# Five 1 KB reads of k, v and the weights on the SP queue of an attention and channel-mix kernel

## The chip, the core and the metric

The kernel runs on one core of a Trainium2 chip. A core has a matrix engine (TensorE, PE in the profile), a vector engine (VectorE, DVE), a scalar engine (ScalarE, ACT), a general engine (GpSimd, POOL) and a queue engine (SyncE, SP) that issues transfers. ACT and POOL can issue transfers too. Sixteen DMA engines carry all transfers between the main memory and the core's working memory. The metric is the device time of one execution in microseconds, lower is better.

## The reference, cut to what matters

Attention without a score matrix, and behind it a channel mix. All inputs are float32: q, k, v of 8 batches x 8 heads x 576 positions x 64, two mixing vectors of 512, and three weights.

```python
q_s = softmax(q, axis=-1)                 # over the 64 of a head
k_s = softmax(k, axis=2)                  # over the 576 positions
kv  = einsum('bhsd,bhse->bhde', k_s, v)   # 64 x 64 for each head
x   = einsum('bhsd,bhde->bhse', q_s, kv)  # put together as 8 x 576 x 512
x_prev = x shifted by one position, a zero row first
xk = mu_k * x + (1 - mu_k) * x_prev
xr = mu_r * x + (1 - mu_r) * x_prev
k  = maximum(xk @ w_k, 0)                 # 512 -> 1024
v  = (k * k) @ w_v                        # 1024 -> 512
out = sigmoid(xr @ w_r) * v
```

w_k is 512 x 1024 (2 MB), w_v 1024 x 512 (2 MB), w_r 512 x 512 (1 MB).

## The kernel before, in words

**Tiling.** A batch's attention is done in two head groups g = 0 and 1 of four heads each (`attention`, L442). For each (batch, group) and each of q, k and v there is one raw tile of 128 x 2 x 576 float32 (576 KB), taken from twelve buffers raw_a to raw_l. Half u = 0 holds two neighbouring heads, half u = 1 the two heads that lie four further; for group 0 these are heads 0, 1 and heads 4, 5. ACT takes the exponentials of q (eq) and k (ek), POOL, ACT or DVE cast v to bf16 (vv), DVE sums and scales q (L467 to L475), PE transposes q (L507) and multiplies k by v (L484). For batches 0 and 1 the mixing with mu is folded into small weights (wp, L564), which need mu spread over all partitions (mu_all); PE multiplies them by q (L520), and DVE and ACT copy the results to xk and xr (L577).

**The channel mix** (`unit`, L694) goes over the positions in pieces of up to 512 columns: w_k matmuls (L722), ReLU on ACT (L706), square on DVE (L710), w_r matmuls (L756) with tanh on ACT (L761), w_v matmuls (L766), the product on DVE (L772), and the stores from SP (L783).

**Loads.** Batch 0's twelve half tiles of 288 KB are loaded from ACT's queue (the q tile of group 0) and from SP's (all others: k and v of group 0, then q, k and v of group 1), by `load` (L301) and the table `FIRST` (L32). SP first issues `emit_mu_rows_load` (L361), two reads of 2 KB each that PE spreads over the partitions (L367), ACT copies (L371) and POOL completes (L375). All other loads, the weights' (cast to bf16 in the transfer) and those of batches 1 to 7, are issued from POOL in the order of `LOADS` (L35) and, behind it, of the batches. The first of them waits until `first[GATE]` has landed, the second half of group 1's q tile (L37, L389, L829).

**The order of the work** comes from a planner (`Plan`, L72). Each operation is added with an engine, a planned time on the engine (`occ`), a planned latency, a key, its dependencies and the buffers it takes and gives. `order` (L133) starts every engine at 0.7 us and always takes the operation that can start first, by the due time (the key, or what its followers leave it) where several can within a look-ahead. Transfers keep their key as due time, so a lower key is an earlier place on the queue. The mu rows have -600 (L378), batch 0's loads -100 to -94.9. The plan treats a transfer of size under 20 as a small one that lands 2.2 us behind its planned end (if its key is negative) and takes no bandwidth; the others share one stream of 404 KB per us that begins 1.75 us behind the issue (`DMA_RATE`, `DMA_LEAD`, L191 to L197):

```python
            if op.size and op.size < 20:
                op.end += 2.2 if op.key < 0 else 6.0
            elif op.size:
                dma_free = max(dma_free, t + DMA_LEAD) + op.size / DMA_RATE
                op.end = dma_free + DMA_TAIL
```

The operations are then emitted sorted by planned start (L205, L827), so the planned times fix the order on each engine and nothing else; on the chip an engine waits for the semaphores of what it needs. Semaphores are assigned to the transfers of SP and ACT in the order of emission.

Of the kernel before, what the change touches and what calls it, by code (L numbers as in the profile page):

```python
# [12 lines left out]
F32 = mybir.dt.float32  # L13
# [195 lines left out]
def kernel(  # L209
# [14 lines left out]
    B, H, S, D = q.shape  # L224
# [16 lines left out]
    plan = Plan(pools, shared)  # L241

    const = ctx.enter_context(tc.tile_pool(name="const", bufs=1))
# [47 lines left out]
    pick = const.tile([2, 2, 64], F32, name="pick")  # L291
    mu_all = const.tile([128, 2, 2, 2, 128], F32, name="mu_all")
    warm = const.tile([1, 1], F32, name="warm")

    copies = {"ACT": nc.scalar.copy, "DVE": nc.vector.tensor_copy, "POOL": nc.gpsimd.tensor_copy}
    queues = {"SP": nc.sync, "ACT": nc.scalar, "POOL": nc.gpsimd}
# [44 lines left out]
    def emit_late_consts():  # L343
        for t in xbs:
            nc.vector.memset(t[:, :, 0:1], 0.0)

    zero = plan.add("DVE", 0.1, 0.15, -10, emit_warm_zero)
    plan.add("ACT", 1.55, 1.6, 3.5, emit_warm, [zero])
    identity = plan.add("POOL", 0.6, 0.8, -9.1, emit_identity)
# [74 lines left out]
    for h in range(2):  # L424
        wv_done.append(plan.add("POOL", 0.8, 0.8, LOADS.index(f"wv{h}"), lambda h=h: emit_wv(h), gate,
                                size=1200.0))
# [434 lines left out]
```

The softmax here doesn't subtract the row's maximum and nothing guards it: scores larger than these inputs give would overflow.

## Time and profile before

| what | us |
|---|---|
| median of 14 runs | 202.36 (201.02 to 203.27) |
| the profiled execution's own time | 201.30 |
| its span, first to last instruction | 199.4 |
| first transfer issued | 0.74 |
| last half of batch 0's group 1 q tile lands | 9.99 |
| first load issued from POOL | 10.29 |
| first w_k matmul (L722) starts | 17.60 |

The span is what the profiler's instructions cover; 1.9 us of the execution's time lie outside it. The profile is of one execution. Its views are: the page, with busy time by engine, the span in slices, the chain of work that ended last and the costliest groups; the windows, with busy time of each engine in a chosen stretch, the granted clock, the share of the DMA engines and GB/s; the waits, with who waited for whom; the instructions in order of time, in which a bracket tells how long the engine had been idle and what released it; and the trace's records of single DMA packets, with start, duration, size and queue, but without the engine or the tile. In a row such as `PE L722 MATMUL` L722 is the line of the kernel. Names ending in q (SPq) are the engines' queues, which issue transfers.

### The profile page before, as it was taken

How to read it: one execution, taken by the hardware profiler on the slowest of the kernel's cores; microseconds unless marked ns; L12 is line 12 of the kernel's file. 1: busy time of each engine (PE TensorE's matmuls, PEld its weight loads, DVE VectorE, ACT ScalarE, POOL GpSimd, SP SyncE). 2: the span in 40 equal slices, each digit the busy share in tenths (PEclk: the TensorE clock that was granted, in tenths of full speed). 3: DMA queues.
4: the chain of work that ended last, by engine and by line, in shares of the span. 5: the costliest groups of instructions: out<-in, count | busy, mean ns of one | idle time of the engine just before them, and what ended most of it. 6: DMA issues, size and time to landing. Idle time of an engine off the chain costs nothing.

```text
span 199.4 us, 5338 instructions
## 1 busy us (share of the span) xinstructions
PE 185.3 (93%) x2171; PEld 96.5 (48%) x2171; DVE 161.0 (81%) x348; ACT 137.3 (69%) x212; POOL 40.4 (20%) x66
## 2 busy tenths in 40 slices
PE   2548999999999999999999999999999999999992
PEld 0234554545444555454576455455455544544761
DVE  2498658898999999999979999999998997432531
ACT  5593795998999699979569978846842752552440
POOL 1494365733444123312300000000000000000000
PEclk9999999999999999999999999999999999999999
DMA  6999999999999999993991220251042204402514
GB/s 200 356 268 198 303 257 340 393 404 409 387 403 408 406 403 384 402 402 93 281 362 31 54 56 0 53 128 35 3 107 56 53 3 105 105 0 57 118 38 105
DMA packets 15520, 40.72 MB, mean 204 GB/s; under 512 B 2300, under 2 KB 3592, under 8 KB 15496
## 3 DMA queue, kind: packets, MB, share of 16 engines
q0 software_dynamic: 7840, 27.40, 40.2%
q1 hardware_dynamic: 7208, 12.26, 21.5%
q10 hardware_dynamic: 448, 0.72, 1.2%
q8 instruction: 17, 0.28, 0.5%
q14 instruction: 7, 0.06, 0.1%
HBM read 33.56 MB, written 9.44 MB: 216 GB/s over the span
## 4 chain that ended last, share of the span: by engine, by line
PE 82%; DMA 12%; DVE 1%; POOL 1%; ACT 0%; issue 0%; SPq 0%; DVEq 0%
PE mm_c L766 11%; PE mm_a L722 9%; PE mm_d L766 8%; PE mm_d L722 8%; PE mm_a L766 7%; PE mm_b L766 6%; PE mm_b L756 6%; PE mm_c L722 6%; PE mm_b L722 5%; DMA wk<-in_moe_w_k_dram 5%; PE mm_d L756 4%; PE mm_a L756 3%; DMA raw_d<-in_q_dram 3%; DMA raw_h<-in_k_dram 3%; PE mm_c L756 3%; PE att_b L520 2%
## 5 line engine op out<-in xcount | busy, mean ns | idle before, releaser
L722 PEld LDWEIGHTS <-wk 128*128 128x128 bf16 x320 | 35.4, 114 | 27.2 <-issue 1.5
L722 PE MATMUL mm_a<-xk,wk 128*128 128x512 bf16 (+1 forms) x100 | 24.5, 359 | 0.0
L722 PE MATMUL mm_d<-xk,wk 128*128 128x512 bf16 (+1 forms) x88 | 22.6, 370 | 0.0
L766 PEld LDWEIGHTS <-k_b 128*128 128x128 bf16 x152 | 14.5, 98 | 15.7 <-issue 0.7
L756 PEld LDWEIGHTS <-xr 128*128 128x128 bf16 x144 | 13.9, 98 | 15.9
L766 PEld LDWEIGHTS <-k_a 128*128 128x128 bf16 x144 | 13.4, 98 | 15.5 <-issue 0.4
L722 PE MATMUL mm_c<-xk,wk 128*128 128x512 bf16 (+1 forms) x68 | 16.4, 362 | 0.0
L722 PE MATMUL mm_b<-xk,wk 128*128 128x512 bf16 (+1 forms) x64 | 15.6, 353 | 0.0
L756 PE MATMUL mm_b<-wr_bf,xr 128*128 128x512 bf16 x52 | 13.4, 379 | 0.0
L766 PE MATMUL mm_c<-wv_bf,k_a 128*128 128x512 bf16 x48 | 12.4, 380 | 0.0
L766 PE MATMUL mm_c<-wv_bf,k_b 128*128 128x512 bf16 x48 | 12.3, 379 | 0.0
L761 ACT ACTIVATE th_a<-mm_b 128x512 f32<-128x512 f32 x12 | 7.1, 595 | 6.4 <-PE mm_b L756 5.3
L766 PE MATMUL mm_d<-wv_bf,k_b 128*128 128x512 bf16 x40 | 10.3, 380 | 0.0
L766 PE MATMUL mm_b<-wv_bf,k_a 128*128 128x512 bf16 x40 | 10.3, 379 | 0.0
L766 PE MATMUL mm_a<-wv_bf,k_b 128*128 128x512 bf16 (+1 forms) x40 | 9.4, 358 | 0.0
L756 PE MATMUL mm_d<-wr_bf,xr 128*128 128x512 bf16 x36 | 9.2, 379 | 0.0
L766 PE MATMUL mm_d<-wv_bf,k_a 128*128 128x512 bf16 x32 | 8.2, 380 | 0.0
L710 DVE TENSOR_TENSOR k_a<-rel_c 128x512 bf16<-128x512 bf16 (+1 forms) x13 | 5.0, 388 | 3.6 <-ACT rel_c L706 3.6
L710 DVE TENSOR_TENSOR k_a<-rel_b 128x512 bf16<-128x512 bf16 (+1 forms) x14 | 5.6, 397 | 2.7 <-ACT rel_b L706 2.7
L761 ACT ACTIVATE th_b<-mm_c 128x512 f32<-128x512 f32 x6 | 3.7, 609 | 5.6 <-PE mm_c L756 4.7
L756 PE MATMUL mm_c<-wr_bf,xr 128*128 128x512 bf16 x28 | 7.2, 379 | 0.0
L756 PE MATMUL mm_a<-wr_bf,xr 128*128 128x512 bf16 x28 | 7.2, 379 | 0.0
(275 smaller groups left out, 416.2 us busy)
## 6 DMA issues: line engine op xcount, KB each, us to landing
out_dram<-ot_a SPq DMA_DIRECT2D x24, 128.0 KB, 3.2
out_dram<-ot_b SPq DMA_DIRECT2D x24, 128.0 KB, 3.2
out_dram<-ot_c SPq DMA_DIRECT2D x22, 128.0 KB, 3.4
raw_b<-in_k_dram POOLq DMA_DIRECT2D x3, 576.0 KB, 8.9
raw_c<-in_v_dram POOLq DMA_DIRECT2D x3, 576.0 KB, 9.1
raw_d<-in_q_dram POOLq DMA_DIRECT2D x3, 576.0 KB, 10.6
raw_a<-in_q_dram POOLq DMA_DIRECT2D x2, 576.0 KB, 10.5
raw_e<-in_k_dram POOLq DMA_DIRECT2D x2, 576.0 KB, 12.3
```

Of the source, the lines that this page charges most:

```text
L520: nc.tensor.matmul(bank(xp)[64 * hf:64 * hf + 64, u, at + c:at + e], lhsT=w[r, hf, :], rhs=qts[qt.index][r, hf, src:src + e - c], start=(n ...
L710: nc.vector.tensor_tensor(out=k2s[k2.index][:, fc, 0:n], in0=rels[rel.index][:, 0:n], in1=rels[rel.index][:, 0:n], op=ALU.mult)
L722: nc.tensor.matmul(bank(kf)[:, 0:n], lhsT=(w[:, h, u, fc % 4:F // 2:4] if split[ct // 2] else w[:, u, F // 2 * h + fc % 4:F // 2 * (h + 1) ...
L756: nc.tensor.matmul(bank(rps), lhsT=xs[1][:, ct, c:c + 128], rhs=wr_bf[:, ct // 2 + 2 * (ct % 2), :], start=(ct == 0), stop=(ct == CT - 1))
L761: nc.scalar.activation(out=ths[th.index][:], in_=bank(rps), func=ACT.Tanh, scale=0.5)
L766: nc.tensor.matmul(bank(vps)[:, 0:w], lhsT=k2s[k2.index][:, ft, 128 * m:128 * m + 128], rhs=wv_bf[:, ft, e:e + w], start=(ft == 0), stop=( ...
```

## The change

A tile of 16 x 5 x 16 float32 is added that nothing reads. A function `touch` issues a read of 16 rows of 64 bytes into it. Five such reads go on SP's queue. Those of k and v have the keys -700 and -699, ahead of the mu rows; their rows lie 8 x 576 elements (18 KB) apart from the tensor's start, so they span the first 288 KB of each. Those of w_k, w_r and w_v have the keys -98.5, -98.49 and -98.48, behind the two halves of group 0's k tile (-99 and -98.9) and ahead of group 0's v tile (-98); their rows are spread over the whole weight, a sixteenth of it apart. Each has a planned time of 0.36 us on SP. The rest of the program text is the same, and no operation depends on the five.

```diff
+    touched = const.tile([16, 5, 16], F32, name="touched")
...
+    def touch(engine, i, src, step):
+
+        return queues[engine].dma_start(out=touched[:, i, :], in_=bass.AP(
+            tensor=src.tensor, offset=src.offset, ap=[[step, 16], [1, 16]]))
+
+    for i, src in enumerate((k, v)):
+        plan.add("SP", 0.36, 0.4, i - 700, lambda i=i, src=src: touch("SP", i, src, 8 * S),
+                 size=10.0)
+    for i, src in enumerate((moe_w_k, moe_w_r, moe_w_v)):
+        plan.add("SP", 0.36, 0.4, 0.01 * i - 98.5, lambda i=i, src=src: touch(
+            "SP", 2 + i, src, src.shape[0] * src.shape[1] // 16), size=10.0)
```

## The prediction

> **What bounds the kernel now.** I read the page's busy shares first, then the windows, then the waits of TensorE, then the chain that ended last, and only then the DMA issues of the first microseconds. The page says that PE is the bound and where it is not yet at work:
>
> ```profile
> span 199.4 us, 5338 instructions
> PE 185.3 (93%) x2171; PEld 96.5 (48%) x2171; DVE 161.0 (81%) x348; ACT 137.3 (69%) x212; POOL 40.4 (20%) x66
> PE   2548999999999999999999999999999999999992
> ```
>
> The third line is PE in 40 slices of 5 us: full from the fifth slice on. The windows put 9.6 us of PE's 14.1 us of idle time ahead of 17.5 us, 3.9 us behind 190 us, and 0.6 us between. So the end moves with the moment at which PE gets going, at 17.60 us with the first k matmul (L722); nothing behind it pays back or adds on its own as long as the loads keep pace. What leads to 17.60 us? The rows of ACT and DVE in time order:
>
> ```profile
> 9.27 1.42 ACT L454 ACTIVATE eq_b<-raw_d 128x576 bf16<-128x576 f32 x2 [1.49 <-DMA raw_d<-in_q_dram]
> ...
> 9.99 1.49 DVE L467 TENSOR_REDUCE rsum_b<-eq_b 128x9 f32<-128x576 bf16 x2 [2.49 <-ACT eq_b L454]
> ```
>
> The brackets are the idle time ahead of each: ACT stood 1.49 us until the q piece of head group 1 (raw_d) landed, DVE 2.49 us until ACT was through. From 9.99 us DVE is busy without a break (2.50 of 2.50 us from 10 to 12.5) up to the mixing weights and the xk copy that PE waits for at 16.50. So **the landing of raw_d is the anchor of the front end**: first half at 9.27, second at 9.99. The second also opens the gate of the POOL loads, as the chain that ended last shows (start, length, what):
>
> ```profile
> 4.03 5.96 DMA raw_d<-in_q_dram
> 9.99 0.30 issue
> 10.29 0.74 POOL raw_g L310
> 11.03 1.41 POOL wk L396 x2
> 12.44 9.08 DMA wk<-in_moe_w_k_dram
> ```
>
> wk's last part lands at 21.52 and PE's first matmul on it starts at 21.64: a margin of 0.12 us. Both paths hang on raw_d.
>
> What sets raw_d's landing is the stream of twelve 288 KB pieces. The windows (the last column is GB/s, the one before it the share of the 16 DMA engines):
>
> ```profile
> 3.50:4.50 1.00, 0.52 (x1) 0.50 (x2) 0.12 (x1) 0.73 (x2) 0.00 (x0) 1.00 1.07 364
> 4.50:5.50 1.00, 1.00 (x2) 0.00 (x0) 0.97 (x2) 0.63 (x1) 0.00 (x0) 1.00 0.93 228
> ...
> 10.50:11.50 1.00, 0.00 (x0) 0.00 (x0) 1.00 (x3) 0.88 (x2) 1.00 (x2) 1.00 1.03 403
> ```
>
> The engines are full from 2.5 us, yet move only 228 GB/s at 4.5 to 5.5 against 403 later. The packet records say why. A 2,304 B packet takes 93 ns, but among the 361 that start from 3.5 to 6.2 us 24 take over 200 (up to 1,115), 12 of 460 from 6.2 to 9.1, and none of 489 after that. The excess is 0.49 + 0.20 us averaged over 16 engines, but over 1 us for the worst one, and a piece lands with its worst engine. These are the first reads of k and v; q's own first reads (1.77 us) cost 14 slow packets of up to 527 ns, 0.23 us averaged. The change goes for these.
>
> One more view is needed, the waits of SP's queue, with its issues:
>
> ```profile
> SPq L310 <- DMA raw_b<-in_k_dram: 0.5, 1, 0.5
> SPq L310 <- DMA raw_a<-in_q_dram: 0.4, 1, 0.4
> ...
> 1.16 0.24 SPq L363 DMA_DIRECT2D mu_rows<-in_moe_mu_r_dram  x1
> 1.44 0.83 SPq L310 DMA_DIRECT2D raw_b<-in_k_dram  x2
> 2.32 0.90 SPq L310 DMA_DIRECT2D raw_c<-in_v_dram  x2
> 3.66 0.80 SPq L310 DMA_DIRECT2D raw_d<-in_q_dram  x2
> ```
>
> SP, issuing, stood 0.4 us from 3.22 to 3.66 for q's landing, which its loads don't read. By the instructions' operands the DMAs of SP and ACT together go round eight semaphores, and the ninth waits for the first to land. Five touches take five of these places.
>
> **The change part by part.** It removes no instruction. It adds five DMA issues on SP and five 1 KB reads, moves every later issue, and may remove slow packets.
>
> *Issues.* A touch has 16 rows; the nearest rows are 0.24 us (mu's second, 2 rows) and 0.36 to 0.43 (128 rows), with 0.05 between. I take 0.25 to 0.30, and 0.36 for SP's first. Before k: touch k 0.74, touch v 1.15, mu 1.45 and 1.73, k's halves at 2.0 and 2.45 to 2.9 (from 1.44 and 1.85). This costs nothing: q's two pieces fill the engines until 3.5 to 4.0, and k's data came at 3.5 at the earliest. The cover is about 0.5 us (2.0 plus about 1.0 from issue to first packet, as q's 0.74 to 1.77).
>
> mu's rows land some 0.5 us later. PE's product on them (L367) (2.04 us) then ends at about 6.45 instead of 6.02; ACT's copy (6.35) and POOL's two products (7.01) slip by up to 0.2, and POOL's casts of v behind them too. The first user is DVE at 13.93: nothing.
>
> *The ring.* By the planned starts the order is q, touch k, touch v, q, mu, mu, k, k: eight. The touch of w_k is the ninth and waits for q's first half (3.65 us). Queued behind it on SP are w_r, w_v, v, v, q, q, k, k, v, v, and everything on the critical path wants q among them. Three touches of 0.30: v's first half is issued at 4.6 instead of 2.32. It is the twelfth, and the fourth (q's second half, landed at 4.4) is done by then. q's halves go at about 5.45 and 5.9 instead of 3.66 and 4.03; the waits for mu and for k's first half (5.7 before) are over.
>
> *What that does to the stream.* k's packets end at 1.77 + 4 x 0.753 (8 packets of 93 ns and one 9 ns semaphore write) = 4.8 plus q's stalls of 0.2 to 0.8, so 5.0 to 5.6 where k has no stalls. v's first data come at 4.6 + 1.0 to 1.1 = 5.65. A hole of 0.1 to 0.65 us. It only costs where an engine would have been earlier: before, the worst engine reached v at about 6.2 (1.77 + 3.01 + 0.35 for q + 1.1 for k).
>
> *The stalls.* With k's and v's stalls gone: 5.65 + 3 x 0.753 + 0.2 left over + 0.37 from last packet to landing = 8.5, against 9.27: **0.8 us gained**. With none gone: the worst engine as before, 9.27: **0**. k's touch reads addresses of heads 0 and 1 alone, while two of the three stalls over 1 us stand at 4.57 and 4.89, when the engines are in heads 4 and 5. Nor is a touch free: an engine's packets follow one another, so a first read that stalls for 0.4 to 1.1 us at 1.7 us holds q's pieces instead of k's.
>
> *The weights' touches.* Before, their first reads stood in the POOL stream: 0.40 us for wk at 12.9, 1.1 to 1.3 at 15.7 to 16.4, 1.5 for wv at 24.8. No PE wait from 12 to 40 us is put down to a weight, so removing them is worth 0 while the margin of 0.12 holds; at best it widens the margin. Now they run at 4.7 to 5.5, on the ring that carries v and q behind them. One stall of 1.1 lets that engine reach v at 5.3 + 1.1 = 6.4: 6.4 + 2.26 + 0.5 (first reads of v and q) + 0.37 = 9.55, **+0.3**. Two on one engine: +1.4. Without any, 0. I take one to two, **+0.8**, since all 16 engines take part in each of three touches.
>
> *The planner.* It orders all engines by planned times, and v's planned start goes from 5.50 to 6.05 (4.30 issue + 1.75 lead), and all behind it by the same 0.55. A shift of everything alike leaves the order; mu's copy keeps its place by the look-ahead (6.46 against 6.49). I take 0. If an order changes, the nearest row is PE's wait for xk of 0.7 us: bounds -0.7 and +0.7.
>
> **A rule of the skill against the change.** The packets read after 33 us, with the engines just as full, hold 10 of 3,193 over twice their usual time: load alone doesn't make them. The Trainium skill's HBM Reference, section Latency, puts an HBM access at 0.2 us on average and 2 us at high load. By that the slow packets would be load, not first reads, no touch could remove any, and the faster case would fall away; by the row they are first reads, and the question is which ones. I go by the row.
>
> **Rivals.** The profiled run took 201.30 us against a median of 202.36, so 1.06 is added to sums on it (0.3%, or 0.6 us, is about what a measurement of this kernel can tell from no change).
>
> 1. *Likeliest, slower:* the ring holds v and q back, the stalls of the weights' first reads land in batch 0's stream, and k's mostly stay. raw_d lands 0.8 later, PE starts 0.8 later, end 202.1 on the profiled run, 203.1 by the median. For it: SP's wait rows, the full DMA engines. Own range 202.9 to 204.2.
> 2. *Faster:* the touches' stalls overlap with q's own at 1.7 us, and later ones fall in the hole. raw_d at 8.5, end 0.8 earlier: 201.6. It decides once the worst engine loses under 0.5 us ahead of v. For it: 24 slow packets just where k and v begin, none by 9.1.
> 3. *It doesn't do what it says:* stalls move from one packet to the next on the same engine, the hole swallows what is saved; raw_d within 0.5 us of 9.27, end 202.4. For it: k's heads 4 and 5 aren't touched.
>
> **How the numbers follow.** Case 1 0.44, case 2 0.32, case 3 0.24; these are also slower, faster and same. Predicted 203.1. Low end: case 2 with 0.4 more for stalls in the k pieces of batch 1, 201.2; high end: two stalls on one engine (+1.4) and half the planner's bound (+0.35), 204.1, and 0.1 for the margin of wk, 204.2.
>
> **What would show it.** SP's queue: the w_k touch starting at about 3.66 with a wait for raw_a, v's first issue at 4.5 or later. In the windows: a dip in the DMA share at 5.0 to 5.7. Packets: fewer or as many over 200 ns from 3.5 to 9.1 us. eq_b's start on ACT: 10.1 in case 1, 8.5 in case 2, about 9.3 in case 3, and PE's first L722 matmul moved by the same amount. I am wrong in the mechanism if that matmul and the end move differently by over 0.5 us: then an order has changed, or a weight is late.

## The result and the profile after

The changed kernel takes a median of 203.91 us in 10 runs (203.12 to 204.39), the kernel before 202.11 us in 47 runs on the same chip. The ratio is 1.0092 with a 95% interval of 1.0071 to 1.0113: **0.9% slower**, about 1.8 us. The profiled execution of the changed kernel took 203.75 us.

The page of the changed kernel, with its span, the busy times and PE in 40 slices:

```profile
span 202.0 us, 5342 instructions
PE 185.3 (92%) x2171; PEld 96.5 (48%) x2171; DVE 160.6 (80%) x348; ACT 136.9 (68%) x212; POOL 40.1 (20%) x66
PE   0528999999999999999999999999999999999991
```

PE's work is the same to a tenth of a microsecond; the span is 2.6 us longer. Read the third line from the left: PE is full from the fifth slice, as before, but the second and third hold 5 and 2 tenths where 5 and 4 stood, and the first none where it held 2. The loss is in the first 20 us. The instructions of ACT in order of time (start, length, what, and the idle time ahead of it):

```profile
6.55 0.68 ACT L466 ACTIVATE ek_a<-raw_b 128x576 bf16<-128x576 f32 x1 [1.42 <-DMA raw_b<-in_k_dram]
...
11.32 1.39 ACT L466 ACTIVATE eq_b<-raw_d 128x576 bf16<-128x576 f32 x2 [3.03 <-DMA raw_d<-in_q_dram]
```

The anchor, eq_b on raw_d, starts at 11.32 instead of 9.27: 2.05 us later, and ACT stands 3.03 us for it instead of 1.49. The first load from POOL goes at 12.30 instead of 10.29, PE's first k matmul (now L734) at 19.61 instead of 17.60:

```profile
12.30 0.74 POOL L311 DMA_DIRECT2D raw_g<-in_q_dram  x1 [1.02 <-DMA raw_d<-in_q_dram]
```

```profile
19.61 1.04 PE L734 MATMUL mm_c<-xk,wk 128*128 128x512 bf16 x2
```

All three moved by 2.01 to 2.05 us. Who held raw_d back stands in the chain of work that ended last (start, length, what; pieces of 0.04 us left out):

```profile
0.74 2.94 DMA raw_a<-in_q_dram
3.71 0.33 SPq L350
...
4.08 0.42 SPq L350
...
4.54 0.42 SPq L350
...
5.00 0.42 SPq L311
...
5.46 0.43 SPq L311
...
5.94 5.36 DMA raw_d<-in_q_dram
```

L350 is the touch. The chain runs from q's first half, which SP waited for, through the three touches of the weights and v's two issues to raw_d's issue: three issues of reads that nobody uses are on the path of the kernel's end. The wait, from SP's waits:

```profile
SPq L350 <- DMA raw_a<-in_q_dram: 0.6, 1, 0.6
```

SP's queue as a whole:

```profile
0.74 0.40 SPq L350 DMA_DIRECT2D touched<-in_k_dram  x1
1.20 0.41 SPq L350 DMA_DIRECT2D touched<-in_v_dram  x1
...
2.28 0.83 SPq L311 DMA_DIRECT2D raw_b<-in_k_dram  x2
3.71 0.33 SPq L350 DMA_DIRECT2D touched<-in_moe_w_k_dram  x1
4.08 0.42 SPq L350 DMA_DIRECT2D touched<-in_moe_w_r_dram  x1
4.54 0.42 SPq L350 DMA_DIRECT2D touched<-in_moe_w_v_dram  x1
5.00 0.89 SPq L311 DMA_DIRECT2D raw_c<-in_v_dram  x2
```

v's first half (raw_c) goes at 5.00 instead of 2.32. The 2.68 us are: 0.84 for the two touches ahead of k (2.28 against 1.44), 0.60 of waiting for q's first half (from 3.11, where k's issues end, to 3.71), and 1.29 for the three touches of the weights (3.71 to 5.00), less a gap of 0.05 that stood ahead of v before. The windows show what the DMA engines did meanwhile (last columns: share of the 16 engines, GB/s):

```profile
3.50:4.50 1.00, 0.00 (x0) 0.00 (x0) 0.07 (x1) 0.74 (x2) 0.00 (x0) 1.00 1.09 336
4.50:5.50 1.00, 0.79 (x1) 0.50 (x2) 1.00 (x2) 0.63 (x1) 0.00 (x0) 1.00 0.78 273
5.50:6.50 1.00, 1.00 (x2) 0.00 (x0) 1.00 (x4) 0.00 (x0) 0.00 (x0) 1.00 0.62 133
6.50:7.50 1.00, 0.52 (x3) 0.13 (x2) 0.99 (x2) 0.95 (x2) 0.00 (x0) 1.00 0.82 293
```

The same window of the kernel before:

```profile
5.50:6.50 1.00, 0.52 (x1) 0.00 (x0) 1.00 (x4) 0.74 (x2) 0.00 (x0) 1.00 0.98 357
```

The share falls to 0.62, and 133 GB/s flow from 5.5 to 6.5 where 357 did. Over the seven windows from 3.5 to 10.5 us the changed kernel moved 1,906 KB and the kernel before 2,466 KB. The 560 KB are worth 1.39 us at 403 GB/s. Their shares differ by 0.98 us (6.11 against 7.09), which is engines without work. The other 0.41 us is work that went more slowly: 48 packets of 2,304 B over 200 ns on SP's queue instead of 36, with an excess of 1.12 us averaged over 16 engines instead of 0.69. The 0.66 us that remain to 2.05 I have not resolved; a piece lands with its worst engine, and these are means.

Behind 20 us the profiled execution loses only one thing more. PE's waits in it have a line that the kernel before does not have:

```profile
PE mm_d L734 <- DVE ot_a L784: 0.5, 1, 0.5
```

It stands at a store that took 6.99 us from 97.39. Matmul by matmul, PE's lag behind the kernel before is 2.01 us at the first k matmul, 1.7 at 45.6 us and 2.3 from 103 us to its last; the two executions differ by 2.45. Most of the loss stands at the start. The medians differ by 1.8, so the 0.5 may be of this one execution.

### The profile page after: what moved, and what is told of

It reads as the page before. It is cut to its first block, busy times and chain, and to the rows that moved or that the text cites. A ratio compares the mean times of both kernels' runs of the same rounds, so it can differ in the third digit from the quotient of the medians.

```text
span 202.0 us, 5342 instructions
## 1 busy us (share of the span) xinstructions
PE 185.3 (92%) x2171; PEld 96.5 (48%) x2171; DVE 160.6 (80%) x348; ACT 136.9 (68%) x212; POOL 40.1 (20%) x66
## 3 DMA queue, kind: packets, MB, share of 16 engines
HBM read 33.57 MB, written 9.44 MB: 213 GB/s over the span
## 4 chain that ended last, share of the span: by engine, by line
PE 85%; DMA 8%; DVE 3%; SPq 1%; ACT 1%; issue 0%; DVEq 0%
PE mm_c L778 10%; PE mm_a L734 9%; PE mm_d L734 9%; PE mm_d L778 7%; PE mm_c L734 7%; PE mm_a L778 7%; PE mm_b L778 6%; PE mm_b L734 6%; PE mm_b L768 5%; PE mm_d L768 4%; DMA out_dram<-ot_a 3%; PE mm_c L768 3%; PE att_b L532 3%; DMA raw_d<-in_q_dram 3%; PE mm_a L768 3%; PE att_a L532 2%
## 5 line engine op out<-in xcount | busy, mean ns | idle before, releaser
L734 PEld LDWEIGHTS <-wk 128*128 128x128 bf16 x320 | 35.4, 114 | 27.8 <-issue 2.1
L734 PE MATMUL mm_a<-xk,wk 128*128 128x512 bf16 (+1 forms) x100 | 24.4, 359 | 0.0
L734 PE MATMUL mm_d<-xk,wk 128*128 128x512 bf16 (+1 forms) x88 | 22.6, 370 | 0.5 <-DVE ot_a L784 0.5
L734 PE MATMUL mm_c<-xk,wk 128*128 128x512 bf16 (+1 forms) x68 | 16.4, 362 | 0.0
L734 PE MATMUL mm_b<-xk,wk 128*128 128x512 bf16 (+1 forms) x64 | 15.6, 353 | 0.0
```

Source lines behind the costliest of these rows:

```text
L734: nc.tensor.matmul(bank(kf)[:, 0:n], lhsT=(w[:, h, u, fc % 4:F // 2:4] if split[ct // 2] else w[:, u, F // 2 * h + fc % 4:F // 2 * (h + 1) ...
```

## The experiments

Two theories were held against each other. **The queue:** five issues and five places among the eight semaphores hold k, v and q back on SP, whatever they read. **The first reads** (the prediction's pricing): packets are slow because they are the first to read a place in memory, and the weights' first reads were moved into batch 0's stream. A third thing to exclude was the size of the touches. Where an edit is to the changed kernel, "after" is named; the others are edits to the kernel before. All were timed in five rounds; the ratio is against the kernel before on the same chip, with the 95% interval.

**1. a_read_q.** After, with all five touches reading from q's first 288 KB.

```diff
-    for i, src in enumerate((k, v)):
+    for i, src in enumerate((q, q)):
...
-    for i, src in enumerate((moe_w_k, moe_w_r, moe_w_v)):
+    for i, src in enumerate((q, q, q)):
...
-            "SP", 2 + i, src, src.shape[0] * src.shape[1] // 16), size=10.0)
+            "SP", 2 + i, src, 8 * S), size=10.0)
```

> All five small reads stand where the change has them, but read q's first 288 KB, which the first load of batch 0 reads anyway. Ring theory (five issues and five places among the eight semaphores hold v and q back, whatever is read): raw_d's first half lands at 11.0 to 11.4, as with the change, and the time is 1.6 to 2.0 us over before (ratio 1.008 to 1.010). Stall theory (the weights' first reads hold the DMA engines up in batch 0's stream): landing at 10.1 to 10.4, 0.8 to 1.1 us over before (1.004 to 1.006).

Measured 203.87 us, ratio 1.0091 (1.0060 to 1.0122): the same as the change. eq_b starts at 11.84, the first k matmul at 20.09 (by its weight load, see number 12), 62 packets take over 200 ns. No weight, no k and no v is touched, and the cost is all there. The stalls of the weights' first reads are not what the change costs.

**2. c_kv_only.** After, without the touches of the weights.

```diff
-    for i, src in enumerate((moe_w_k, moe_w_r, moe_w_v)):
-        plan.add("SP", 0.36, 0.4, 0.01 * i - 98.5, lambda i=i, src=src: touch(
-            "SP", 2 + i, src, src.shape[0] * src.shape[1] // 16), size=10.0)
```

> Only the touches of k and v, ahead of the mu rows. v's first half is then the ninth transfer and waits for q's first half, so it is issued at 3.7 and its data come at 4.8, ahead of the end of k's packets at about 5.1. Ring theory: no hole, 0 to 0.2 us over before. Stall theory: 0, or faster by up to 0.8 us if the two touches take k's and v's slow packets away.

Measured 203.31, ratio 1.0057 (1.0032 to 1.0082), eq_b at 10.62. That is about 1.15 us, where both theories said 0 to 0.2 or a gain. I had thought that an issue of k delayed by 0.85 us is covered by q's two pieces; in this profile it is not, ek_a starts 0.90 us later (6.66 against 5.76). Whether that costs anything at the end, number 10 tells. With two places of the ring taken, v now waits for q's first half and goes at 3.79 instead of 2.32, raw_d at 4.63. In this kernel POOL also does v's cast ahead of the mu products, so the order of one engine changed as well.

**3. d_weights_only.** After, without the touches of k and v.

```diff
-    for i, src in enumerate((k, v)):
-        plan.add("SP", 0.36, 0.4, i - 700, lambda i=i, src=src: touch("SP", i, src, 8 * S),
-                 size=10.0)
```

> Only the three weights' touches, at the place of the change. The third of them is the ninth transfer and waits for q's first half (3.65), v's first half is issued at about 4.1, 0.9 us earlier than with the change, its data come at 5.2 to 5.4. Ring theory: 0.3 to 0.6 us over before. Stall theory: 0.8 to 1.1 us or more over before, with packets of over 1 us on SP's queue from 5 to 9 us.

Measured 203.19, ratio 1.0057 (1.0032 to 1.0083), eq_b at 10.26; k goes at 1.44 as before, v at 3.97, raw_d at 4.91. This is about 1.15 us, the cost that the text above gives to the stall theory, and two packets of 1.82 and 1.93 us stand where it puts them. But number 9, without a touch, has four of 1.07 to 1.42 us, so such packets are no sign of the weights' reads. Each part costs 0.57% and both together 0.92%. The delays of raw_d's issue add up (0.97 and 1.25 us against 2.28); whether the costs do, the intervals leave open.

**4. h_weights_late.** The touches of the weights alone, behind all of batch 0's loads on SP.

```diff
-        plan.add("SP", 0.36, 0.4, 0.01 * i - 98.5, lambda i=i, src=src: touch(
+        plan.add("SP", 0.36, 0.4, 0.01 * i - 94, lambda i=i, src=src: touch(
```

> Only the three weights' touches, behind all of batch 0's loads on SP, where they hold nothing of batch 0 back and still land ahead of the weights' loads. Ring theory: raw_d lands as before, 0 to 0.1 us over before. Stall theory: the same, or faster by what the weights' slow packets cost before, at most 0.3 us, since no wait of TensorE was put down to a weight.

Measured 202.44 against 202.09, ratio 1.0009 (0.9984 to 1.0034). ACT's row of the anchor:

```profile
9.17 1.44 ACT L463 ACTIVATE eq_b<-raw_d 128x576 bf16<-128x576 f32 x2 [1.78 <-DMA raw_d<-in_q_dram]
```

It is at 9.17, where it was before (9.27). Issued at 7.72 to 9.48, with nothing of batch 0 behind them, the same three reads cost nothing that can be measured, and they bring nothing.

**5. e_pool_touch.** After, with all five touches issued from POOL.

```diff
-        plan.add("SP", 0.36, 0.4, i - 700, lambda i=i, src=src: touch("SP", i, src, 8 * S),
+        plan.add("POOL", 0.3, 0.3, i - 8.5, lambda i=i, src=src: touch("POOL", i, src, 8 * S),
...
-        if op.engine == "POOL" and op.size and gate:
+        if op.engine == "POOL" and op.size and op.key >= 0 and gate:
```

(The three weights likewise, with keys from -6.5.)

> The five touches of the change, same addresses, issued from POOL's queue from about 1.3 us on, while POOL is idle, so that SP's queue is as before. Queue theory (the change costs by holding SP's queue, and touching is worth nothing): raw_d's first half lands at 9.1 to 9.4, 0 to 0.2 us over before. First-read theory (touches do take slow packets away, the queue hides it): raw_d at 8.5 to 8.9, fewer than 20 packets over 200 ns on SP's queue up to 9 us, 0.4 to 0.8 us faster than before.

Measured 201.45 against 201.59, ratio 0.9992 (0.9967 to 1.0017), eq_b at 9.44. The same five reads from another queue are free. POOL issued them from 1.47 to 4.08, but their packets ran only from 4.4 us on, behind k's first ones, so this is no test of what an early touch of k could bring. The Trainium skill, page "DMA: Bandwidth & Descriptors", section "Issuing engines are not separate DMA queues", says that starting transfers from several engines saves only the issuing sequencer's time, "usually small relative to the DMA itself". This pair of runs agrees with the first half. The second does not hold here: what the five reads cost on SP is their issue time of 0.33 to 0.42 us each and their places among the semaphores, 0.92% against nothing from POOL; the pair does not separate the two.

**6. x1_one_region.** Before, with all twelve loads of batch 0 reading the same 288 KB of q.

```diff
-            ap = bass.AP(tensor=src.tensor,
-                         offset=src.offset + (b * H + 2 * g + 4 * u.start) * S * D,
+            ap = bass.AP(tensor=src.tensor if b else q.tensor,
+                         offset=(src.offset + (b * H + 2 * g + 4 * u.start) * S * D
+                                 if b else q.offset),
```

> Part of the computation is changed: all twelve loads of batch 0 read the same 288 KB of q, so nothing behind the first of them is read for the first time; issues, places and sizes are those of before. First-read theory: no slow packets behind 3.5 us, raw_d's first half at 8.0 to 8.4, 0.8 to 1.1 us faster. If the slow packets have another cause: as many as before (30 or more over 200 ns on SP's queue), raw_d at 9.1 to 9.5, within 0.2 us of before.

The result is no longer the reference's, since batch 0 reads q in place of k and v. Measured ratio 1.0001 (0.9974 to 1.0029), eq_b at 9.42. This is the sharpest test of the first reads, since k's and v's packets here read addresses that q's have read already. From 3.5 to 6.2 us 29 of the 319 packets on SP's queue take over 200 ns, up to 1,416; before it was 24 of 331, up to 1,115 (the 361 of the prediction count ACT's queue too). Number 12 says the same from the other side: there k and v are read for the first time, and one of 287 is slow. **The slow packets are not first reads**, and a touch had nothing to take away. The prediction's row was read wrongly.

**7. x3_mu_pool.** Before, with the mu rows issued from POOL, so that SP begins with k.

```diff
-            nc.sync.dma_start(out=mu_rows[:, m, :], in_=bass.AP(
+            nc.gpsimd.dma_start(out=mu_rows[:, m, :], in_=bass.AP(
...
-    rows_load = plan.add("SP", 0.9, 0.9, -600, emit_mu_rows_load, size=10.0)
+    rows_load = plan.add("POOL", 0.3, 0.3, -9.05, emit_mu_rows_load, size=10.0)
...
+        if op.engine == "POOL" and op.size and op.key >= 0 and gate:
```

> The opposite of the change: no touches, and the two mu rows go from SP's to POOL's queue, which frees two of the eight places and 0.7 us of SP. k's first half is issued at 0.74, v's at 1.6, raw_d's at 2.5 and 2.9 without a wait. Queue theory: raw_d follows its issue, by up to the stream's limit (1.77 + 7 x 0.753 + 0.9 of stalls + 0.37 = 8.3): 8.3 to 8.9, 0.4 to 0.9 us faster than before. If the DMA stream and not the issue sets raw_d: 9.2 to 9.4, 0 to 0.2 us.

Measured 203.12 against 201.59, ratio 1.0064 (1.0039 to 1.0089): slower, though the stream became faster. SP issued k at 0.74, v at 1.65 and raw_d at 2.69, without a wait. Only 10 packets on its queue took over 200 ns (excess 0.25 us), and 383 GB/s flowed from 4.5 to 5.5 us. But ACT works in order, and this row stands ahead of eq_b:

```profile
9.70 0.59 ACT L371 COPY mu_all<-mm_a 128x512 f32<-128x512 f32 x1 [2.78 <-PE mm_a L367]
```

The mu rows from POOL reached PE at about 7.6 us. ACT waited 2.78 us for PE's product with them, and eq_b followed at 10.77. The experiment says nothing on what an earlier raw_d is worth at the end, since it added a wait, and much on the stream.

**8. x6_hold_v.** Before, without a touch; v's first half waits on SP for q's second half.

```diff
+        if op is first[4]:
+            tc.add_manual_dep(op.made.ins, first[1].made.ins.name, sync)
```

> No touches and no added transfer; v's first half waits on SP for q's second half (landed at about 4.4), so v goes at 4.4 and 4.9, raw_d at 5.3 and 5.8, 0.6 us less than the change's delay. Queue theory: raw_d's first half at 10.6 to 11.2, 1.2 to 1.7 us over before (ratio 1.006 to 1.008), with a hole in the DMA share at 5.1 to 5.5 and as many or more slow packets behind it. If the transfers themselves cost and not the delay: within 0.3 us of before.

Measured 202.43 against 201.59, ratio 1.0032 (1.0007 to 1.0058). v goes at 4.36, raw_d at 5.21. The first half of raw_d landed early (eq_b at 8.90), the second late (11.07), and with it the POOL gate (11.35) and the first k matmul (18.64). Holding v back is enough to make the kernel slower, by about 0.65 us where 1.2 to 1.7 were expected.

**9. s7_hold_less.** The same wait on q's first half, which is the wait that the ring makes.

```diff
+        if op is first[4]:
+            tc.add_manual_dep(op.made.ins, first[0].made.ins.name, sync)
```

> No touches; v's first half waits on SP for q's first half (landed at about 3.65), so v is issued at 3.65 and 4.1 and raw_d at 4.6 and 5.05, while k keeps its place: the delay of v and q that two added transfers behind k bring through the ring, without the transfers. If the delay alone costs: between before and the hold to 4.36, 0.2 to 0.5 us over before. If data for v still come ahead of the end of k's packets (4.65 against 5.1): 0 to 0.2 us.

Measured 202.72 against 201.90, ratio 1.0039 (1.0014 to 1.0064), about 0.8 us and more than either expectation. SP's rows of v and raw_d, then, by another view, ACT's row of the anchor:

```profile
3.73 0.80 SPq L310 DMA_DIRECT2D raw_c<-in_v_dram  x2
4.58 0.91 SPq L310 DMA_DIRECT2D raw_d<-in_q_dram  x2
```

```profile
10.24 1.47 ACT L454 ACTIVATE eq_b<-raw_d 128x576 bf16<-128x576 f32 x2 [3.03 <-DMA raw_d<-in_q_dram]
```

raw_d is issued 0.92 us later than before and lands 0.97 later. The delay went through whole, though the engines were at a share of 1.0 until 6.5 us; only from 6.5 to 7.5 did it fall, to 0.81 with 217 GB/s.

**10. s6_kv_behind_k.** After, with the touches of k and v alone, moved behind k's halves: SP then issues v and q at the times of the run above.

```diff
-        plan.add("SP", 0.36, 0.4, i - 700, lambda i=i, src=src: touch("SP", i, src, 8 * S),
+        plan.add("SP", 0.36, 0.4, 0.01 * i - 98.5, lambda i=i, src=src: touch("SP", i, src, 8 * S),
...
-    for i, src in enumerate((moe_w_k, moe_w_r, moe_w_v)):
-        plan.add("SP", 0.36, 0.4, 0.01 * i - 98.5, lambda i=i, src=src: touch(
-            "SP", 2 + i, src, src.shape[0] * src.shape[1] // 16), size=10.0)
```

> Only the touches of k and v, now behind k's two halves, so that k and the mu rows keep their times of before and v is issued at 3.65 or a little later, as with the hold to q's first half, but with two small transfers ahead of it in the queue. If the place ahead of k was what cost with the two touches alone (1.15 us): as with that hold, 0.2 to 0.5 us over before. If small transfers ahead of the bulk cost by themselves: 0.8 to 1.2 us, with 10 or more packets over 600 ns.

Measured 202.95, ratio 1.0056 (1.0029 to 1.0084), with v at 3.68, raw_d at 4.54 and eq_b at 10.41, against 3.73, 4.58 and 10.24 with the bare wait. The cost of about 1.1 us is what the text above gives to the small transfers themselves; but the bare wait cost 0.8 too, with 10 packets over 600 ns against 9 here. The intervals overlap: with equal issue times the touches' own transfers add nothing that these runs can tell. Against number 2 (1.0057), where v and raw_d go within 0.11 us of these times and k 0.85 us later, the place ahead of k adds nothing that shows either.

**11. s3_rows512.** After, with rows of 512 B instead of 64 B.

```diff
-    touched = const.tile([16, 5, 16], F32, name="touched")
+    touched = const.tile([16, 5, 128], F32, name="touched")
...
-            tensor=src.tensor, offset=src.offset, ap=[[step, 16], [1, 16]]))
+            tensor=src.tensor, offset=src.offset, ap=[[step, 16], [1, 128]]))
```

> The change with rows of 512 bytes in place of 64, all else equal. If the short rows disturb the DMA engines (a write of under 512 bytes): fewer than 8 packets over 600 ns on SP's queue and 0.4 to 0.8 us less than the change. If it is the number and the place of the issues: the same as the change, 1.6 to 2.0 us over before.

Measured 203.67, ratio 1.0093 (1.0057 to 1.0129): the cost of the change again. A 64 B packet takes 8 to 11 ns in the changed kernel; the touches' bytes and rows are not the cost.

**12. x7_mu_pool_late.** Number 7 with the planner told of the late mu rows, so that ACT takes eq_b ahead of their copy. It was the one candidate for a kernel better than both.

```diff
-    rows_load = plan.add("POOL", 0.3, 0.3, -9.05, emit_mu_rows_load, size=10.0)
+    rows_load = plan.add("POOL", 0.3, 4.1, -9.05, emit_mu_rows_load, size=10.0)
```

> No touches; the mu rows on POOL's queue, and the planner told that they land 4 us later, so that ACT and PE no longer stand waiting for them in the middle of batch 0. The loads of SP are issued 0.7 us earlier than before and raw_d has no wait. Queue theory: raw_d's first half at 8.2 to 8.8, first w_k matmul 0.4 to 1.0 us earlier, 0.4 to 1.0 us faster than before. If the mu rows still come too late for the weights of the mixing, or if the DMA stream sets raw_d: within 0.3 us of before.

Measured 201.80 against 201.90, ratio 0.9991 (0.9968 to 1.0014): no difference. The early issue did its work: 15 packets over 200 ns, excess 0.29 us. A window of the stream:

```profile
4.50:5.50 1.00, 0.00 (x0) 0.00 (x0) 0.06 (x1) 0.78 (x2) 0.00 (x0) 1.00 1.05 389
```

389 GB/s flow where the kernel before had 228, and eq_b starts at 8.45, 0.82 us earlier. Where did the gain go? DVE's rows, in order of time:

```profile
9.16 1.52 DVE L467 TENSOR_REDUCE rsum_b<-eq_b 128x9 f32<-128x576 bf16 x2
...
10.84 1.88 DVE L475 TENSOR_TENSOR qs_b<-eq_b,rrec_b 128x576 bf16<-128x576 bf16 x2
12.64 0.74 DVE L460 CAST vv_b<-raw_f 128x576 bf16<-128x576 f32 x1
```

rsum_b and qs_b start 0.83 and 0.81 us earlier than before. Then qs_b takes 1.88 us instead of 1.42, and what follows is 0.34 earlier (12.64 against 12.98, the last xk copy 16.96 against 17.30). So 0.47 us went to a longer qs_b, and 0.35 reach PE: the weight load of the first k matmul starts at 17.25 against 17.60. (The matmul's own record is missing here, as in all twelve experiments: they have 2,147 matmul records, the two main kernels 2,171. So "first k matmul" means its weight load in the experiments; in the two main kernels both start together.) Then the gain is gone at once. The fifth and sixth k matmul, in the kernel before and, by another view, here:

```profile
20.03 0.62 PE L722 MATMUL mm_a<-xk,wk 128*128 128x512 bf16 x2
```

```profile
20.19 0.99 PE L722 MATMUL mm_a<-xk,wk 128*128 128x512 bf16 x2
```

A pair takes about 1.05 us up to 18.44 and 0.62 from 20.03 there; here still 0.99 at 20.19 and 0.60 from 21.01. The eighth k matmul starts at 21.23 against 20.71. From the first to the eighth pass 3.11 us in the profile before, 3.98 here, also 3.98 in number 6, and 3.07 to 4.21 over the fourteen profiles. So the moment at which PE goes over to the faster pace differs between profiles by more than the gain looked for; what sets it no run here shows. A gain of 0.35 us lies inside the interval (0.65 us faster to 0.28 slower).

**The runs together.** By the issue of raw_d's first half on SP, each from one profile, without the two kernels whose mu rows come late:

| kernel | k, v, raw_d issued, us | eq_b, us | first k matmul (its weight load), us | packets over 200 ns, excess us | ratio |
|---|---|---|---|---|---|
| h_weights_late | 1.44, 2.32, 3.58 | 9.17 | 17.52 | 29, 0.65 | 1.0009 |
| before | 1.44, 2.32, 3.66 | 9.27 | 17.60 | 36, 0.69 | 1 |
| e_pool_touch | 1.44, 2.32, 3.75 | 9.44 | 17.73 | 23, 0.50 | 0.9992 |
| x1_one_region | 1.45, 2.32, 3.76 | 9.42 | 17.76 | 36, 0.63 | 1.0001 |
| s6_kv_behind_k | 1.44, 3.68, 4.54 | 10.41 | 18.77 | 33, 0.91 | 1.0056 |
| s7_hold_less | 1.45, 3.73, 4.58 | 10.24 | 18.61 | 28, 0.88 | 1.0039 |
| c_kv_only | 2.29, 3.79, 4.63 | 10.62 | 18.96 | 38, 1.15 | 1.0057 |
| d_weights_only | 1.44, 3.97, 4.91 | 10.26 | 18.54 | 50, 1.26 | 1.0057 |
| x6_hold_v | 1.45, 4.36, 5.21 | 8.90 (2nd half 11.07) | 18.64 | 34, 0.66 | 1.0032 |
| s3_rows512 | 2.29, 4.84, 5.78 | 10.57 | 19.33 | 61, 1.40 | 1.0093 |
| a_read_q | 2.28, 4.98, 5.92 | 11.84 | 20.09 | 62, 1.70 | 1.0091 |
| after | 2.28, 5.00, 5.94 | 11.32 | 19.61 | 48, 1.12 | 1.0092 |

The ratios fall into three groups by issue time alone: up to 3.76 us none, 4.54 to 5.21 some 0.3 to 0.6%, 5.78 to 5.94 0.9%. What the five transfers read and how long their rows are makes no difference that shows. In the middle group the three kernels with touches lie at 0.56 to 0.57% and the two without at 0.32 and 0.39%, inside each other's intervals, so a small price of the transfers themselves is not excluded. In ten of the twelve kernels eq_b starts 5.35 to 5.99 us behind raw_d's issue, wherever that stands; 4.79 us in s3_rows512 and 3.69 in x6_hold_v, whose second half came late, are the exceptions. The queue theory holds for most of the cost, the first reads fall.

## Why the prediction was right or wrong

It forecast 203.1 with a range of 201.2 to 204.2 and its likeliest case as slower by the ring; measured 203.91. The direction, the mechanism of the ring and the path to the end were right. The size came from a wrong term, and that 203.91 lies in the range is in part luck: the 0.8 us of the forecast stood on the weights' first reads, the upper end on two such stalls and a changed order, and the runs show neither.

- *What bounds the kernel*: right. eq_b, the POOL gate and the first k matmul moved by 2.05, 2.01 and 2.01 us, and the executions by 2.45; the test of the mechanism (matmul and end within 0.5 us of each other) is met by a hair by the executions (0.44) and just missed by the spans (which differ by 2.53, so 0.52), because of the 0.5 us at 97 us.
- *Issues*: too short, and half covered. A touch of 16 rows was put at 0.25 to 0.30 us, 0.36 for SP's first; it takes 0.40 to 0.42, and 0.33 right after a wait. k's issue went 0.84 later instead of 0.5, and ek_a, which follows its first half's landing, started 0.79 later (6.55 against 5.76), so q's pieces did not cover it; in number 11, with k issued at the same time, they did (5.83). "This costs nothing" is not refuted by that: numbers 2 and 10 differ in k's place and cost the same.
- *mu's rows*: PE's wait for them is 4.7 us instead of 4.0; ACT's copy and POOL's products slip by 0.79 instead of up to 0.2, since ek_a stands ahead of the copy. No later wait of PE was put down to them, so they cost nothing, as said.
- *The ring*: right in kind. The touch of w_k waits for q's first half and starts at 3.71 (said 3.66), v's issue is at 5.00 (said 4.6), raw_d's at 5.94 (said 5.45). The 0.4 to 0.5 us too little are the issues' length above. The wait for k's first half, said to be over by then, held raw_d's second half until 6.54 (said 5.9).
- *What that does to the stream*: **this step failed.** The hole was to cost only where an engine would have been earlier, because its worst engine reached v at 6.2 anyway. So raw_d's issue 1.8 us later (5.45 against 3.66) was given no price of its own: without new stalls the landing stayed at 9.27, and the 0.8 came from the next term but one. On the chip 2.28 us of issue became 2.05 of landing, and in number 9, 0.92 became 0.97; over the eight kernels with a later raw_d it is 0.6 to 1.4 us of landing for each us of issue (the second half's landing in number 8). The engines' backlog covered little of a late issue.
- *The stalls*: the first reads of k and v are none (number 6), so the faster case had nothing to stand on. The count of slow packets even rose, from 36 to 48.
- *The weights' touches*: the +0.8 that made the forecast was priced as stalls of the weights' first reads. Number 1 has no weight's read and the same cost. No run shows this term; what they show in its place is the step above, with 2.05 us.
- *The planner*: right, no order changed on PE, ACT, DVE or POOL.
- *The rule weighed*: I put the Trainium skill's HBM Reference, section Latency (0.2 us on average, 2 us at high load) aside for the reading as first reads. Number 6 takes that reading away. It does not make load alone the cause either: in number 12 the engines moved 389 to 409 GB/s in each microsecond from 3.5 to 7.5 and had one packet over 200 ns among SP's 287 from 3.5 to 6.2, against 24 of 331 before, at a lower rate.

## What to carry to other kernels

A read that nobody waits for still has a price: its issue time on the queue (0.4 us here) and its place among the queue's semaphores, both paid by whatever stands behind it; so list what is issued behind it before pricing its bytes, and put it on a queue, or at a place, with nothing urgent behind. The full transfer stream absorbed little of a late issue here: price the landing as moved by as much as the issue until a run shows less. And test a cause such as "the first read is slow" by changing the address alone (number 6), which costs one run and no argument. Before explaining an idle time that is put down to "issue", count the records: in number 12 it was a matmul that the profile lacks.

## What the runs showed of the hardware that was not expected

**Transfers issued early ran faster.** Where SP began with k at 0.74 us (numbers 7 and 12) the excess of packets over 200 ns was 0.25 and 0.29 us; with k at 1.44 and v at 2.32 it was 0.50 to 0.69, with v alone held back, by touches or by a wait, 0.66 to 1.26, with k at 2.28 too 1.12 to 1.70. These are single profiles, and in the first two the mu rows had left the queue as well, so depth of the queue, the mu rows and chance are not told apart. In number 12, 13 of the 15 slow packets on SP's queue start before 2.5 us, beside q's first ones. What makes the packets slow stays open. Part of it may be the restart of an engine without work: of the 24 packets that start from 5.95 to 6.27 us, when v's first data come behind the hole, 10 took 233 to 647 ns. Not tried was the ring by itself, with places taken but no issue time.

**A transfer from POOL landed late beside a full hardware queue.** The mu rows were issued from POOL at 1.46 and 2.12 us and reached PE at about 7.6, where from SP, issued at 0.74 and 1.16, they had reached it at about 4.0.

**DVE and POOL slowed each other.** In number 12, qs_b took 1.88 us while POOL did its two mu products (10.79 to 12.11), and 1.42 before, when POOL only issued loads. The fourteen profiles show it again at qs_a, two DVE products with two bf16 inputs each, beside POOL's two mu products. Where the two don't overlap, as in the changed kernel, the pairs take 1.42 and 0.77 to 0.78 us. Where they do, one or both are longer. In number 10, DVE's row and, by another view, POOL's:

```profile
6.67 1.62 DVE L484 TENSOR_TENSOR qs_a<-eq_a,rrec_a 128x576 bf16<-128x576 bf16 x2
```

```profile
6.86 1.69 POOL L384 TENSOR_SCALAR mu_all<-mu_all 128x256 f32<-128x256 f32 x2 [5.56 <-ACT mu_all L380]
```

In the kernel before POOL alone lost (1.13 us, qs_a 1.42); in numbers 3, 6, 8, 9 and 10 both did (qs_a 1.61 to 1.62, the mu products 1.31 to 1.69). The Trainium skill's page "SBUF — State Buffer", section "SBUF: two separate sides", says that DVE with two inputs from that memory and POOL share a port pair as an exclusive lock; the rows agree in direction, and number 12 loses 0.46 us on DVE and 0.55 on POOL. No run here separates the port from other causes.
